# Key maxima as an activation bias, query maxima crossed by DMA, queries rounded by a reduction: an attention and feed-forward kernel on one core

## The chip, the cores and the metric

The kernel runs on one core of one Trainium2 chip. The metric is the device time of the whole program in microseconds, as the median of several runs. A profiled execution, recorded by the hardware, gives the start and the length of every instruction on the five engines: TensorE (PE, with its weight loads shown as PEld), VectorE (DVE), ScalarE (ACT), GpSimd (POOL) and SyncE (SP), which here only issues transfers.

## The reference

Attention with a feature map in place of the softmax, followed by two dense layers:

```python
def phi(x):                                   # x: [8, 8, 576, 64], w_phi: [64, 128]
    proj = np.einsum('bhsd,df->bhsf', x, w_phi)
    proj = proj - np.max(np.abs(proj), axis=-1, keepdims=True)
    return np.concatenate([np.exp(proj), np.exp(-proj)], axis=-1)
q_p, k_p = phi(q), phi(k)
kv = np.einsum('bhsf,bhsd->bhfd', k_p, v)
z = np.sum(k_p, axis=2)
num = np.einsum('bhsf,bhfd->bhsd', q_p, kv)
den = np.einsum('bhsf,bhf->bhs', q_p, z)[..., None] + 1e-06
x = (num / den)   # heads side by side: [4608, 512]
h = x @ w_in      # [512, 2048]
out = np.maximum(0.01 * h, h) @ w_out         # [2048, 512]
```

All in float32. For every token (key or query) the largest absolute value over its 128 projected features is subtracted before the exponentials. The second half takes the exponential of the negated difference, that is of maximum minus projection.

## The kernel before

The work of attention is cut into 32 pairs: a pair is two heads of one batch, and four pairs make a batch of 576 tokens. Pairs 0 to 3 have a route of their own (`first_k_phase`, `first_q_phase`). Pairs 4 to 31 go through `k_phase(i)` and `q_phase(i)`, generators that yield between their steps. `attention()` interleaves the key phase of pair i with the query phase of pair i - 1, step by step.

Precise matrix products are made of rounded ones: a float32 value is split into a rounded high part and the rest (`kph` and `kpl` from `ek`, `qh` and `ql` from `eq`, `gh` and `gl` from `g`), and each product is three matmuls. Before pair 8 (`nat` in the code, `NK` and `NN` being 8) the phases use float32 matmuls and no split.

The key phase goes over the tokens in three groups `g` (two chunks of 128 tokens, two more, and one of 64). Tokens lie on the partitions, features along the free axis, so a token's maximum `m4` is a VectorE reduction (L252), one column for each chunk and head. The subtraction of the maximum is `ksub` (through the helper at L72, on VectorE, VectorE and POOL in turn, as `ENG` says), two exponentials follow for each chunk on ScalarE (L262 and L263, `ek`), then the split and the matmuls into `kvp` (L224). At the end `kvh` and `kvl` are written for the query phase. `kvh` has one buffer, so this waits until the query phase before has read it.

The query phase has features on the partitions after its matmuls (L337, L338). A VectorE transpose of 32x32 blocks (L339) turns the features of each group of 32 partitions along the free axis (`tq`), and a reduction (L341) gives, for each of four partition groups, the maximum over its own 32 features: `m`, of 128 partitions by 2 heads by 18 blocks of tokens. The maximum of a token is that over the four groups, so `m` has to cross partitions: six small VectorE operations (L343 to L348) fold the upper half on the lower, then the second quarter on the first, and copy the result back to all four. Then come, for each head, the subtraction (L354), the transpose back (L356), the exponentials (L361, L362), the split into `qh` (a cast, in the helper at L69) and `ql`, the matmuls with `kvh` and `kvl` (L376 to L381), and the copies of numerator and denominator (L383, L384). A last part transposes the denominators, takes reciprocals and multiplies into `ring` (L387 to L390 and L72). `tq`, `m`, `ms`, `mb` and `rc` have one buffer each, so two query phases hardly overlap.

`ring` holds two batches of attention's output. The feed-forward layers take blocks of 256 tokens from it, 18 in all: `split(i)` makes `xh` and `xl`, `layer1` (L562 to L565) the 16 groups of 128 hidden features, each followed by an activation and a split (`g`, `gh`, `gl`), and `layer2` (L582 to L584) adds them up in `acc`, from where the result is copied and stored (L590). A block needs whole batches: block 4 the pairs up to 11, block 6 those up to 15. The weights are loaded and split between the first stage and about 210 us (`load_weights`, L169).

The order of instructions on each engine is fixed when the program is built. A planner runs through the work with priorities and its own estimate of each instruction's time; attention (`PA`) comes ahead of the weights (`PW`), and these ahead of the feed-forward layers (0). On the chip every engine, and SP's queue of transfers, then works through its list in that order, and each instruction waits for what it needs.

Of the kernel before, what the change touches and what calls it, by code (L numbers as in the profile page):

```python
# [9 lines left out]
F32 = mybir.dt.float32  # L10
# [3 lines left out]
AF = mybir.ActivationFunctionType  # L14
ALU = mybir.AluOpType
AX = mybir.AxisListType

P = 128
B, H, S, D = 8, 8, 576, 64
NP = H // 2  # L20
F = 128
# [23 lines left out]
def attention_moe_kernel(ctx: ExitStack, tc: tile.TileContext, q, k, v, vt, w_phi, w_in, w_out, out):  # L45
    nc = tc.nc
# [7 lines left out]
    def st(shape, dt, tag):  # L54
        return sp.tile(shape, dt, tag=tag, name=tag, bufs=BUFS.get(tag, 1))
# [8 lines left out]
    def copy_(key, o, i):  # L64
        e = pick(key) or "a"
        if e == "a":
            nc.scalar.copy(o, i)  # L67
        else:
            (nc.vector if e == "v" else nc.gpsimd).tensor_copy(o, i)  # L69

    def tt_(key, o, a, b, op):
        (nc.vector if pick(key) == "v" else nc.gpsimd).tensor_tensor(o, a, b, op=op)  # L72
# [132 lines left out]
    def k_phase(i):  # L205
        nat = i < NK
        rk, rv = kraw.pop(i)
        if not nat:
            ks = st([P, 2, S], F32R, "ks")
            for j in range(2):  # L210
                o, n = slice(64 * j, 64 * j + 64), slice(64 - 64 * j, 128 - 64 * j)
                copy_("kh", ks[o, j], rk[o])
                nc.vector.tensor_tensor(ks[n, j], rk[o], ks[o, j].bitcast(F32), op=ALU.subtract)  # L213
            vh, vl = values()
            copy_("vh", vh[:, :, 0:64], rv[:, :, 0:64])
            for r, c in ((slice(0, P), slice(0, 8)), (slice(64, P), slice(8, 10))):
                tt_("vl", vl[r, c], rv[r, c, 0:64], vh[r, c, 0:64].bitcast(F32), ALU.subtract)
        if i + 1 < B * NP:
            load_k(i + 1)
        yield  # L220
        kvp = pt("c")

        def kv_mm(j, lt, rt, first=False, last=False):
            nc.tensor.matmul(kvp[0 : lt.shape[1], 256 * j : 256 * j + 256], lhsT=lt, rhs=rt,  # L224
                             start=first and j == 0, stop=last, skip_group_check=True)

        for g in range(3):
            w = 2 if g < 2 else 1
            r = slice(0, P) if g < 2 else slice(64, P)
            n = P if g < 2 else 64  # L230
            m4 = st([P, 4], F32, "m4")
            pmk = st([P, 4, F], F32, "pmk")
            if nat:
                pk = pt("a")
                for s in range(w):
                    t0 = (2 * g + s) * P if g < 2 else S - P
                    proj(pk, s, rk[:, t0 : t0 + P])
                pkv = pk[r, 0 : 256 * w].rearrange("p (a f) -> p a f", f=F)
            else:
                for s in range(w):  # L240
                    t0 = (2 * g + s) * P if g < 2 else S - P
                    pk = pt("a")
                    for j in range(2):
                        nc.tensor.matmul(pk[:, 256 * j : 256 * j + 256], lhsT=ks[:, j, t0 : t0 + P],
                                         rhs=wq.rearrange("p a f -> p (a f)"), start=True, stop=True)
                    pk = pk[r].rearrange("p (j x f) -> p j x f", j=2, x=2)
                    x = pmk[r, 2 * s : 2 * s + 2]
                    copy_("pk", x, pk[:, :, 1])
                    nc.vector.tensor_tensor(x, pk[:, :, 0], x, op=ALU.add)
                    yield  # L250
                pkv = pmk[r, 0 : 2 * w]
            nc.vector.tensor_reduce(m4[r, 0 : 2 * w], pkv, axis=AX.X, op=ALU.max, apply_absolute_value=True)  # L252
            mb = m4[r, 0 : 2 * w].unsqueeze(2).broadcast_to([n, 2 * w, F])
            if nat:
                nc.vector.tensor_tensor(pmk[r, 0 : 2 * w], pkv, mb, op=ALU.subtract)
            else:
                tt_("ksub", pkv, pkv, mb, ALU.subtract)
            yield
            for s in range(w):
                c = 2 * g + s  # L260
                ek = st([P, 2, 256], F32, ("ek", "kph", "kpl")[c % 3] if nat else "ek")
                nc.scalar.activation(ek[r, :, 0:F], pmk[r, 2 * s : 2 * s + 2], AF.Exp)  # L262
                nc.scalar.activation(ek[r, :, F:256], pmk[r, 2 * s : 2 * s + 2], AF.Exp, scale=-1.0)  # L263
                if nat:
                    for j in range(2):
                        kv_mm(j, rv[r, 4 * j + c if c < 4 else 8 + j], ek[r, j], first=c == 0, last=c == 4)
                    yield
                    continue
                if c < 4:
                    kph = st([P, 2, 256], F32R, "kph")  # L270
                    kpl = st([P, 2, 256], F32R, "kpl")
                    copy_("kph", kph, ek)
                    tt_("kpl", kpl, ek, kph.bitcast(F32), ALU.subtract)
                    for j in range(2):
                        kv_mm(j, vh[:, 4 * j + c], kph[:, j], first=c == 0)
                        kv_mm(j, vl[:, 4 * j + c], kph[:, j])
                    for j in range(2):
                        kv_mm(j, vh[:, 4 * j + c], kpl[:, j])
                else:
                    kst = st([P, 2, 256], F32R, "kph")  # L280
                    copy_("kst", kst[r], ek[r])
                    nc.vector.tensor_tensor(kst[0:64], ek[r], kst[r].bitcast(F32), op=ALU.subtract)
                    for j in range(2):
                        kv_mm(j, vl[:, 8 + j], kst[:, j])
                        kv_mm(j, vh[:, 8 + j], kst[:, j], last=True)
                yield
        kvs = st([P, 2, 256], F32, "ek").rearrange("p a (b f) -> p a b f", b=2)[0:66]
        copy_("kvs", kvs, kvp[0:66].rearrange("p (a b f) -> p a b f", a=2, b=2))
        yield
        kvt = pt("c")  # L290
        kvtv = kvt[:, 0:264].rearrange("p (a b f) -> p a b f", a=2, b=2)
        for j in range(2):
            for t in range(2):
                nc.tensor.transpose(kvtv[:, j, t], kvs[:, j, t], ident[0:66, 0:66])
        if i < NN:
            kvh = st([P, 2, 2, P], F32, "kvh")
            nc.scalar.copy(kvh[:, :, :, 0:64], kvtv[:, :, :, 0:64])
            nc.scalar.copy(kvh[:, :, :, 64:P], kvtv[:, :, :, 64:65].broadcast_to([P, 2, 2, 64]))
            kvs_of[i] = kvh, None
        else:  # L300
            kvh = st([P, 2, 2, P], F32R, "kvh")
            kvl = st([P, 2, 2, P], F32R, "kvl")
            zb = kvtv[:, :, :, 64:65].broadcast_to([P, 2, 2, 64])
            copy_("kvh", kvh[:, :, :, 0:64], kvtv[:, :, :, 0:64])
            copy_("kvh", kvh[:, :, :, 64:P], zb)
            nc.vector.tensor_tensor(kvl[:, :, :, 0:64], kvtv[:, :, :, 0:64], kvh[:, :, :, 0:64].bitcast(F32), op=ALU.subtract)
            nc.vector.tensor_tensor(kvl[:, :, :, 64:P], zb, kvh[:, :, :, 64:P].bitcast(F32), op=ALU.subtract)
            kvs_of[i] = kvh, kvl
        yield
# [4 lines left out]
    def q_phase(i):  # L314
        b, hp = divmod(i, NP)
        nat = i < NN
# [12 lines left out]
        for j in range(2):  # L329
# [9 lines left out]
                nc.vector.transpose(tq[:, j, u], pq)  # L339
                yield  # L340
            nc.vector.tensor_reduce(m[:, j], blocks(tq[:, j]), axis=AX.X, op=ALU.max, apply_absolute_value=True)  # L341
        ms = st([64, 2, 18], F32, "ms")
        nc.vector.tensor_copy(ms, m[64:128])  # L343
        nc.vector.tensor_tensor(m[0:64], m[0:64], ms, op=ALU.max)
        nc.vector.tensor_copy(ms[0:32], m[32:64])
        nc.vector.tensor_tensor(m[0:32], m[0:32], ms[0:32], op=ALU.max)
        nc.vector.tensor_copy(m[32:64], m[0:32])
        nc.vector.tensor_copy(m[64:128], m[0:64])  # L348
        yield
        kvh, kvl = kvs_of[i]  # L350
        dn = tq[:, 0]
        for j in range(2):
# [6 lines left out]
            for u in range(2):  # L359
                eq = st([P, 2, U], F32, "eq")  # L360
                nc.scalar.activation(eq[:, 0], mb[:, u], AF.Exp)  # L361
                nc.scalar.activation(eq[:, 1], mb[:, u], AF.Exp, scale=-1.0)  # L362
                if nat:
                    es.append((eq, None))
                else:
                    qh = st([P, 2, U], F32R, "qh")
                    ql = st([P, 2, U], F32R, "ql")
                    copy_("qh", qh, eq)
                    tt_("ql", ql, eq, qh.bitcast(F32), ALU.subtract)
                    es.append((qh, ql))  # L370
                yield
# [307 lines left out]
```

## Time and profile before

| | us |
|---|---|
| Median of 3 runs | 1229.77 (1229.44 to 1230.68) |
| Profiled execution, its time | 1229.39 |
| its span, first to last instruction | 1227.6 |
| TensorE matmuls busy | 1179.4 (96%) |
| VectorE busy | 839.9 (68%) |
| ScalarE busy | 795.7 (65%) |
| POOL busy | 665.8 (54%) |
| TensorE clock granted, mean | 0.995 |

Busy times count an engine's instructions without its waits. Matmuls overlap one another, so 96% is not the share of the peak. Rows of groups read: line, engine, operation, output and inputs by the program's names, shapes, count, then busy us and mean ns, then the idle time before them and what ended it. Rows of a single line give shortest, median and longest in ns and the first and last start in us. L69 and L72 are helpers, so those rows are told apart by their tiles. SPq rows are issues of transfers by SP's queue.

### The profile page before, as it was taken

To read this page: it belongs to the slowest core of one execution; us is meant where nothing else is said; L and a number is where in the kernel's file an instruction comes from. 1 tells how busy PE (TensorE), PEld (TensorE's weight loads), DVE (VectorE), ACT (ScalarE), POOL (GpSimd) and SP (SyncE) were. 2 spreads that over 40 slices of the span, in tenths; PEclk is the share of its full clock that TensorE was granted. 3 is DMA by queue.
4 is the path that set the end of the run, shared out by engine and by line. 5 is a ranking of instruction groups with operands and counts; after the bars stand their busy time and mean duration, and the time that the engine had idled before them with its cause. 6 is when DMAs were issued, how large, how long until landed. Compare 5 with 4: busy or idle time off the path is not lost. (4 is left out here: it accounts for less than half of the span.)

```text
span 1227.6 us, 21133 instructions
## 1 busy us (share of the span) xinstructions
PE 1179.4 (96%) x7496; PEld 1033.1 (84%) x7496; DVE 839.9 (68%) x1359; ACT 795.7 (65%) x2027; POOL 665.8 (54%) x705
## 2 busy tenths in 40 slices
PE   8889999899998999999999999999999999999998
PEld 5577778788886889899898998889988889998997
DVE  6969995687887788888788888825888887200000
ACT  5977775776675676777777776745776766433232
POOL 0131222567665576768668785645677866433232
PEclk9999999999999999999999999999999999999999
DMA  7525231211111101111111111110111100000000
GB/s 211 147 75 174 82 105 30 75 30 32 38 31 48 31 28 41 30 40 32 48 32 48 24 47 30 42 28 29 30 49 31 35 14 1 19 18 1 18 18 18
DMA packets 62777, 57.00 MB, mean 46 GB/s; under 512 B 45136, under 2 KB 46288, under 8 KB 62672
## 3 DMA queue, kind: packets, MB, share of 16 engines
q1 hardware_dynamic: 62672, 55.65, 16.1%
q8 instruction: 59, 0.97, 0.3%
q14 instruction: 46, 0.38, 0.1%
HBM read 46.20 MB, written 9.44 MB: 45 GB/s over the span
## 5 line engine op out<-in xcount | busy, mean ns | idle before, releaser
L72 POOL TENSOR_TENSOR gl<-g,gh 128x256 fp32r<-128x256 f32 x288 | 242.0, 843 | 300.1 <-ACT gh L67 232.3
L562 PE MATMUL h<-xh,w0h 128*128 128x256 f32 x1088 | 278.4, 284 | 4.0 <-ACT xh L67 1.7
L563 PE MATMUL h<-xh,w0l 128*128 128x256 f32 x1088 | 276.3, 282 | 0.0
L562 PEld LDWEIGHTS h<-xh,w0h 128*128 128x128 f32 x1088 | 205.6, 189 | 16.1 <-ACT xh L67 2.3
L582 PE MATMUL acc<-w1h,gh 128*128 128x512 f32 x544 | 216.3, 398 | 2.2 <-DVE o L69 1.5
L583 PE MATMUL acc<-w1l,gh 128*128 128x512 f32 x544 | 214.8, 395 | 0.0
L563 PEld LDWEIGHTS h<-xh,w0l 128*128 128x128 f32 x1088 | 205.6, 189 | 8.6
L584 PE MATMUL acc<-w1h,gl 128*128 128x512 f32 x544 | 205.4, 396 | 1.2 <-POOL gl L72 1.2
L569 ACT ACTIVATE g<-h 128x256 f32<-128x256 f32 x288 | 109.1, 382 | 135.0 <-PE h L565 90.1
L72 POOL TENSOR_TENSOR ql<-eq,qh 128x576 fp32r<-128x576 f32 x96 | 154.8, 1618 | 65.9 <-DVE qh L69 57.4
L565 PE MATMUL h<-xl,w0h 128*128 128x256 f32 x1088 | 189.0, 283 | 0.3 <-POOL xl L72 0.2
L67 ACT CAST gh<-g 128x256 fp32r<-128x256 f32 x288 | 114.9, 403 | 66.2 <-PE acc L583 64.2
L565 PEld LDWEIGHTS h<-xl,w0h 128*128 128x128 f32 x1088 | 155.3, 190 | 2.4 <-POOL xl L72 1.9
L72 POOL TENSOR_TENSOR kpl<-ek,kph 128x512 fp32r<-128x512 f32 x72 | 102.2, 1420 | 38.2 <-ACT kph L67 17.2
L69 DVE CAST qh<-eq 128x576 fp32r<-128x576 f32 x96 | 97.2, 1016 | 36.0 <-ACT eq L362 22.7
L584 PEld LDWEIGHTS acc<-w1h,gl 128*128 128x128 f32 x544 | 100.1, 188 | 19.6 <-POOL gl L72 2.2
L582 PEld LDWEIGHTS acc<-w1h,gh 128*128 128x128 f32 x544 | 102.5, 188 | 16.2 <-DVE o L69 2.5
L583 PEld LDWEIGHTS acc<-w1l,gh 128*128 128x128 f32 x544 | 102.5, 188 | 11.5
L361 ACT ACTIVATE eq<-mb 128x288 f32<-128x288 f32 x112 | 49.2, 439 | 77.3 <-DVE mb L356 73.8
L69 DVE COPY o<-acc 128x512 f32<-128x512 f32 x16 | 10.7, 672 | 124.0 <-DMA out_dram<-o 124.0
L262 ACT ACTIVATE ek<-pmk 128x256 f32<-128x256 f32 (+1 forms) x128 | 53.4, 417 | 61.5 <-DVE pmk L72 19.6
L224 PE MATMUL c<-kph,vhl 128*66 128x256 f32 (+1 forms) x480 | 77.9, 284 | 6.1 <-ACT kph L67 3.3
(205 smaller groups left out, 2444.6 us busy)
## 6 DMA issues: line engine op xcount, KB each, us to landing
out_dram<-o SPq DMA_DIRECT2D x35, 256.0 KB, 2.0
rq<-in_q_dram SPq DMA_DIRECT2D x28, 288.0 KB, 2.9
rk<-in_k_dram SPq DMA_DIRECT2D x27, 288.0 KB, 2.8
rv<-in_v_dram SPq DMA_DIRECT2D x29, 256.0 KB, 3.5
ring<-in_w_in_dram SPq DMA_DIRECT2D x9, 512.0 KB, 3.9
f<-in_w_out_dram SPq DMA_DIRECT2D x7, 512.0 KB, 3.6
f<-in_w_in_dram SPq DMA_DIRECT2D x7, 512.0 KB, 3.7
ring<-in_w_out_dram SPq DMA_DIRECT2D x5, 512.0 KB, 3.6
```

Source lines behind the costliest of these rows:

```text
L67: nc.scalar.copy(o, i)
L69: (nc.vector if e == "v" else nc.gpsimd).tensor_copy(o, i)
L72: (nc.vector if pick(key) == "v" else nc.gpsimd).tensor_tensor(o, a, b, op=op)
L224: nc.tensor.matmul(kvp[0 : lt.shape[1], 256 * j : 256 * j + 256], lhsT=lt, rhs=rt, start=first and j == 0, stop=last, skip_group_check=True)
L262: nc.scalar.activation(ek[r, :, 0:F], pmk[r, 2 * s : 2 * s + 2], AF.Exp)
L562: nc.tensor.matmul(ph, lhsT=weight(0, "h", ft)[:, d * P : d * P + P], rhs=xh[d], start=d == 0, stop=False)
L563: nc.tensor.matmul(ph, lhsT=weight(0, "l", ft)[:, d * P : d * P + P], rhs=xh[d], start=False, stop=False)
L565: nc.tensor.matmul(ph, lhsT=weight(0, "h", ft)[:, d * P : d * P + P], rhs=xl[d], start=False, stop=d == NP - 1)
L569: nc.scalar.activation(g, ph, AF.Prelu, alpha=0.01)
L582: nc.tensor.matmul(a, lhsT=gh[:, ts], rhs=weight(1, "h", ft), start=ft == 0, stop=False)
L583: nc.tensor.matmul(a, lhsT=gh[:, ts], rhs=weight(1, "l", ft), start=False, stop=False)
L584: nc.tensor.matmul(a, lhsT=gl[:, ts], rhs=weight(1, "h", ft), start=False, stop=ft == NFT - 1)
```

## The change

In the key phase, from pair 8 on, the subtraction goes away. VectorE negates the maxima (`m4n`), and the exponentials take maximum or negated maximum as a bias per token, which needs an activation for each head: four of 128 elements for each chunk in place of two of 256. In the query phase of all pairs from 4 on, the four partition groups' maxima are brought side by side on 32 partitions by four transfers on SP's queue, reduced by one VectorE instruction, and sent to all four groups by four more transfers; `ms`, `mm` and `mx` have one buffer each, and there is one more yield. From pair 8 on the rounding of `eq` to `qh` is a VectorE maximum over an axis of one element instead of a cast.

```diff
@@ k_phase
             mb = m4[r, 0 : 2 * w].unsqueeze(2).broadcast_to([n, 2 * w, F])
+            if not nat:
+                m4n = st([P, 4], F32, "m4n")
+                nc.vector.tensor_scalar(m4n[r, 0 : 2 * w], m4[r, 0 : 2 * w], -1.0, None, op0=ALU.mult)
             if nat:
                 nc.vector.tensor_tensor(pmk[r, 0 : 2 * w], pkv, mb, op=ALU.subtract)
-            else:
-                tt_("ksub", pkv, pkv, mb, ALU.subtract)
             yield
             for s in range(w):
...
-                nc.scalar.activation(ek[r, :, 0:F], pmk[r, 2 * s : 2 * s + 2], AF.Exp)
-                nc.scalar.activation(ek[r, :, F:256], pmk[r, 2 * s : 2 * s + 2], AF.Exp, scale=-1.0)
+                if nat:
+                    nc.scalar.activation(ek[r, :, 0:F], pmk[r, 2 * s : 2 * s + 2], AF.Exp)
+                    nc.scalar.activation(ek[r, :, F:256], pmk[r, 2 * s : 2 * s + 2], AF.Exp, scale=-1.0)
+                else:
+                    for j in range(2):
+                        h = 2 * s + j
+                        nc.scalar.activation(ek[r, j, 0:F], pmk[r, h], AF.Exp, bias=m4n[r, h : h + 1])
+                        nc.scalar.activation(ek[r, j, F:256], pmk[r, h], AF.Exp, scale=-1.0, bias=m4[r, h : h + 1])
@@ q_phase
-        ms = st([64, 2, 18], F32, "ms")
-        nc.vector.tensor_copy(ms, m[64:128])
-        nc.vector.tensor_tensor(m[0:64], m[0:64], ms, op=ALU.max)
-        nc.vector.tensor_copy(ms[0:32], m[32:64])
-        nc.vector.tensor_tensor(m[0:32], m[0:32], ms[0:32], op=ALU.max)
-        nc.vector.tensor_copy(m[32:64], m[0:32])
-        nc.vector.tensor_copy(m[64:128], m[0:64])
+        ms = st([32, 4, 2, 18], F32, "ms")
+        for a in range(4):
+            nc.sync.dma_start(ms[:, a], m[32 * a : 32 * a + 32])
+        yield
+        mm = st([32, 2, 18], F32, "mm")
+        nc.vector.tensor_reduce(mm, ms.rearrange("p a j c -> p j c a"), axis=AX.X, op=ALU.max)
+        mx = st([P, 2, 18], F32, "mx")
+        for a in range(4):
+            nc.sync.dma_start(mx[32 * a : 32 * a + 32], mm)
+        m = mx
         yield
...
-                    copy_("qh", qh, eq)
+                    nc.vector.tensor_reduce(qh, eq.unsqueeze(3), axis=AX.X, op=ALU.max)
                     tt_("ql", ql, eq, qh.bitcast(F32), ALU.subtract)
```

## The prediction

> **What bounds the kernel now.** I read the page's busy shares first, then stages cut out of the trace, then what each engine waited for, then single stretches of the timeline.
>
> ```profile
> span 1227.6 us, 21133 instructions
> PE 1179.4 (96%) x7496; PEld 1033.1 (84%) x7496; DVE 839.9 (68%) x1359; ACT 795.7 (65%) x2027; POOL 665.8 (54%) x705
> ...
> 92.10:122.80 30.70, 30.70 (x173) 23.73 (x172) 28.40 (x56) 24.44 (x55) 5.82 (x9) 1.00 0.60 174
> 368.40:399.10 30.70, 25.40 (x145) 20.66 (x145) 22.59 (x37) 16.20 (x42) 17.27 (x20) 0.94 0.17 48
> 399.10:798.20 399.10, 388.40 (x2602) 350.02 (x2600) 338.31 (x515) 288.69 (x748) 282.27 (x270) 1.00 0.14 36
> 798.20:828.90 30.70, 29.85 (x203) 27.10 (x202) 8.27 (x12) 14.74 (x37) 15.12 (x17) 1.00 0.09 24
> ```
>
> The window rows give length, then PE, PEld, DVE, ACT, POOL busy (and counts), granted clock, DMA share, GB/s. TensorE is busy nearly throughout and its work is not touched, so by the shares alone the change could win at most the stalls. Two rows say more. From 798 to 829 VectorE falls to 8.27 of 30.70 us while PE goes on: attention has run ahead and waits for room in the ring. From 368 to 399 it is the other way: PE gets through 145 matmuls where the long stage after it has 2602 in 399.1 us, 200 in the same time, and its clock is granted at 0.94. There PE is short of tokens:
>
> ```profile
> 235.28 1.42 POOL L72 TENSOR_TENSOR ring<-ring,mb 128x576 f32<-128x576 f32 x1 [2.17 <-ACT o L67]
> 236.84 0.35 ACT L67 CAST xh<-ring 128x192 fp32r<-128x192 f32 x1
> 380.07 1.41 POOL L72 TENSOR_TENSOR ring<-ring,mb 128x576 f32<-128x576 f32 x1 [0.20 <-DVE mb L390]
> 381.51 0.30 ACT L67 CAST xh<-ring 128x128 fp32r<-128x128 f32 x1 [0.22 <-POOL ring L72]
> 381.87 0.39 PE L562 MATMUL h<-xh,w0h 128*128 128x256 f32 x1 [1.02 <-ACT xh L67]
> 515.00 1.43 POOL L72 TENSOR_TENSOR ring<-ring,mb 128x576 f32<-128x576 f32 x1
> 516.46 0.24 ACT L67 CAST xh<-ring 128x64 fp32r<-128x64 f32 x1 [0.80 <-POOL ring L72]
> ```
>
> The last product of pair 7, of pair 11 and of pair 15 is split for the feed-forward layers the moment it is there (236.84, 381.51, 516.46), and at 381.87 PE waited for that split. So up to pair 15 the end of each batch of attention paces PE; later PE paces attention, with the 30 us pause at 798 as slack.
>
> Attention's own pace is that of the query phase. It has one `tq`, so a pair starts when the one before is done:
>
> ```profile
> 1035.33 0.48 DVE L339 STREAM_TRANSPOSE tq<-a 128x288 f32<-128x288 f32 x1
> 1057.49 0.78 DVE L390 STREAM_TRANSPOSE mb<-rc 128x576 f32<-128x576 f32 x1
> L390 DVE STREAM_TRANSPOSE mb<-rc x28: 728/778/779, 133.7 to 1057.5; 128x576 f32<-128x576 f32 x28
> ```
>
> The last transposes (L390) of 28 query phases lie 27 steps apart from 133.7 to 1057.5 us: 34.2 us a pair, about 33.1 without the pause. Pair 31, the only one with no key phase beside it, takes 1035.3 to 1058.3, 23 us. So some 10 us a pair are lost to sharing engines with the next pair's keys.
>
> **The change, part by part.** The rows are those of 245 to 1045 us (pairs 8 to 31, nearly).
>
> ```profile
> L72 DVE TENSOR_TENSOR pmk<-pmk,m 128x512 f32<-128x512 f32 x46 | 41.9, 910 | 0.7
> L72 POOL TENSOR_TENSOR pmk<-pmk,m 64x256 f32<-64x256 f32 x23 | 16.1, 699 | 24.7 <-DVE m L252 18.6 <-PE a L244 2.4 <-ACT tq L384 2.4
> L262 ACT ACTIVATE ek<-pmk 128x256 f32<-128x256 f32 x92 | 38.5, 418 | 38.9 <-DVE pmk L72 19.6 <-POOL kpl L72 18.6
> L67 ACT CAST xh<-ring 128x128 fp32r<-128x128 f32 x16 | 3.7, 296 | 0.2 <-POOL ring L72 0.2
> L345 DVE COPY ms<-m x28: 170/172/1200, 109.1 to 1039.6; 32x36 f32<-32x36 f32 x28
> L343 DVE COPY ms<-m 64x36 f32<-64x36 f32 x24 | 9.0, 373 | 0.4
> L345 DVE COPY ms<-m 32x36 f32<-32x36 f32 x24 | 11.3, 470 | 0.8
> L348 DVE COPY m<-m 64x36 f32<-64x36 f32 x24 | 8.9, 370 | 0.8
> L69 DVE CAST qh<-eq 128x576 fp32r<-128x576 f32 x96 | 97.2, 1016 | 36.0 <-ACT eq L362 22.7
> L69 DVE CAST qh<-eq x96: 434/907/1702, 257.1 to 1049.5; 128x576 fp32r<-128x576 f32 x96
> L341 DVE TENSOR_REDUCE m<-tq x56: 702/749/756, 96.8 to 1038.4; 128x18 f32<-128x576 f32 x56
> ```
>
> *Keys.* Per pair the subtraction goes: 2 of 0.91 us on VectorE and one of 0.70 us on POOL. In its place come 3 negations `m4n` of 2 or 4 columns. The nearest row is the small copy L345: 0.17 us at best and in the middle, 0.47 on average over the stage, up to 1.2 when something holds it up. I take 0.4, so VectorE gains 1.8 - 1.2 = 0.6 us a pair (bounds 0.4 and 1.3). ScalarE goes from 2 instructions a chunk of 256 elements (0.418 each) to 4 of 128 (0.296 for a 128-element cast): 1.18 for 0.84, +0.35 a chunk, +1.7 us a pair of 5 chunks. ScalarE has 288.69 of 399.1 us busy, 24 us a pair, so it can carry that; it lies in the key phase, which waits for the query phase at `kvh`. Price 0 on the path. The Trainium skill ("ScalarE: Activation LUTs", section "What ACT_TABLE_LOAD costs") adds about 93 ns for a bias read per partition; no row here has one. By it the surcharge would be about 3.6 us a pair, an estimate from that page, and ScalarE still not full.
>
> *Rounding of the queries.* 4 casts a pair, 0.43 to 1.70 us, median 0.91, mean 1.02, become reductions. A reduction over the same 576 elements costs 0.75 us and hardly varies. -0.27 us each, -1.1 a pair on the query path from pair 8 on; an undisturbed cast (0.43) loses 0.3 each, so the bounds are -1.1 and +1.2.
>
> *The crossing.* Out go the six small operations L343 to L348, 0.37 to 0.47 us each on average (first, dearest and last are shown), together 2.46 us of VectorE a pair, in all 28 pairs. In come 4 DMAs, a reduction of 144 elements on 32 partitions (between the 0.17 us of a small copy and the 0.75 of 576 elements; I take 0.3), 4 DMAs. Both hops lie on the query path: `m` to `ms` to `mm` to `mx` to L354. All eight go through SP's queue; behind them stand the loads of the next pair and the stores of the output.
>
> ```profile
> rv<-in_vt_dram SPq DMA_DIRECT2D x58, 32.0 KB, 2.9
> out_dram<-o SPq DMA_DIRECT2D x35, 256.0 KB, 2.0
> L191 SPq DMA_DIRECT2D rk<-in_k_dram x26: 327/334/436, 12.9 to 964.8; - x26
> L193 SPq DMA_DIRECT2D rv<-in_vt_dram x28: 658/662/1505, 23.5 to 977.6; - x28
> 388.62 0.34 SPq L200 DMA_DIRECT2D rq<-in_q_dram  x1
> 391.02 0.56 SPq L192 DMA_DIRECT2D rv<-in_v_dram  x1
> 391.63 0.67 SPq L193 DMA_DIRECT2D rv<-in_vt_dram  x1
> 388.52 0.71 DVE L343 COPY ms<-m 64x36 f32<-64x36 f32 x1
> 391.49 0.18 DVE L348 COPY m<-m 64x36 f32<-64x36 f32 x1
> ```
>
> SP spends 0.33 to 0.66 us on an issue, and a transfer lands 2.0 (the stores) to 2.9 us (the smallest loads) after its issue starts. The last of four issues starts 3 x 0.33 = 1.0 to 3 x 0.66 = 2.0 us after the first, so a hop is 3.0 to 4.9 us; I take 4.0, the middle. Crossing: 2 x 4.0 + 0.3 = 8.3, bounds 6.3 and 10.1. Pair 12's crossing (388.52 to 391.67) falls together with the loads for the next pair on SP (388.62 to 392): a load waiting for its buffer holds the small DMAs behind it, and they hold the loads. I add 1 us: 9.3 in place of 2.5 of work, +6.8 on the path.
>
> While the hop runs, VectorE is free for the key phase. That gives back part of the 10 us of sharing. I take 3.5, half of the 6.8 us hole: VectorE is busy for 28 us a pair (338.31 of 399.1 us, 33.1 a pair), but the hole can only take key work that is ready in it. So from pair 8: +6.8 - 1.1 - 3.5 - 0.6 = +1.6 us a pair (bounds -2 and +6).
>
> Pairs 4 to 7 have no rounding gain, VectorE stays full there (28.40 of 30.70 at 92 us), and SP's queue also feeds the weights, whose loads wait for staging room:
>
> ```profile
> SPq L169 <- DVE ql L177: 66.7, 22, 5.8
> PE a L376 <- DVE qh L69: 4.3, 8, 0.9
> PE a L337 <- DVE tq L339: 3.1, 4, 1.3
> PE c L224 <- POOL kpl L72: 2.4, 6, 0.8
> ```
>
> That is 3 us for each of 22 loads (66.7 in total). The hole there is filled with weight work, which PE needs too. I take +3.5 us a pair, half of the 6.8 (bounds 0 and +10, with a 3 us load ahead of each hop).
>
> **The sum.** Up to pair 15 this reaches PE: 4 x 3.5 + 8 x 1.6 = 27 us. From there 16 x 1.6 = 26 us fits into the 30 us pause. What comes back: PE stalls on VectorE and POOL (4.3 + 3.1 + 2.4 us in the last rows and smaller ones), and slowed chains once PE itself runs short; I take -8. Span 1227.6 + 27 - 8 = 1246.6. The profiled execution took 1229.39, 1.8 over its span and 0.4 under the median of 1229.77: 1248.4, on the median's scale 1248.8. I say 1248.
>
> **The rivals.** *The hop is short and VectorE's relief decides (faster).* VectorE loses 2.46 - 0.3 + 1.1 + 0.6 = 3.9 us of its 28 a pair. If the crossing takes 6.3 us, the lower bound, and the key work fills the hole, the path loses 3.8 - 1.1 - 3.5 - 0.6 = -1.4 us a pair. The first 12 pairs can give at most what PE lost waiting for tokens: between 368 and 399 some 55 matmuls of 0.15 us, 8.4 us, and less at pairs 7 and 15. With the 8 of stalls that is 1230 - 17 = 1213; about half of it, 1221, is likelier. For it: the six small operations cost 2.46 us where six undisturbed ones (0.17) would cost 1.0, so much of VectorE's time is waiting that goes with them. It decides once the crossing is below some 7.7 us, where the +1.6 above is used up. The Trainium skill ("SBUF — State Buffer", section "Who interferes with whom") has a copy, a cast and a two-input operation fight POOL for a shared port, and a reduction never; the trace agrees (casts 0.43 to 1.70, reductions 0.70 to 0.76), and by that rule alone the change should win. By the same page the negations can still be held up. Chance 0.29.
>
> *It all hides (same).* The key work fills the hole exactly and PE, 96% busy, sees nothing: within 2.5 us, 0.2%, about what a measurement of this kernel can tell from no change. Against it: pairs 7, 11 and 15. Chance 0.08.
>
> *VectorE's order does not leave the room (much slower).* Engines run in a fixed order. If the reduction on `ms`, and L354 on `mx`, stand in VectorE's order 2 us too early each, everything behind them waits: the key phase's L249, the transposes L339, then PE. +4 us a pair over my +1.6: 5.6 x 12 = 67 in the first half plus the part of 90 in the second that the pause of 30 does not take, partly repaid as PE's shortage frees ScalarE and POOL: some 1265 to 1320, by how much of it is repaid. Nothing here shows how the order reckons with a small DMA. Chance 0.18.
>
> **How the numbers follow.** Likeliest: the crossing lengthens attention moderately, 1233 to 1265, chance 0.45, at 1248 (the likeliest case's own range). Slower is 0.45 + 0.18 = 0.63, same 0.08, faster 0.29. For 8 in 10 I cut the lower part of the fast case (below 1214) and the upper part of the slow one (above 1290): 1214 to 1290.
>
> **What would show it.** Right: VectorE's total near 840 - 28 x 2.2 - 96 x 0.27 - 14 = 738 us; the `qh` reductions at 0.75 us; ScalarE up by 40 to 90 us; from the end of the second L341 to L354 8 to 11 us; 35 to 36 us a pair; PE's clock dipping near pairs 7, 11 and 15 for longer than now. Wrong: a crossing under 7 us, or pairs that follow each other in 32 us, would make it faster; `mm` waiting on SP behind loads for 5 us and more, or VectorE idle at `mm` and L354 with key work behind it, much slower.

## The result and the profile after

The changed kernel takes 1221.51 us (median of 5 runs), the kernel before 1230.68 in the same series: a ratio of 0.9926, 95% interval 0.9913 to 0.9939. I had forecast 1248, slower. The profiled execution has a span of 1217.5 us, 10.1 less than before.

The page of the changed kernel, and below it the stages (length, then PE, PEld, DVE, ACT, POOL busy with counts, granted clock, DMA share, GB/s), first of the kernel before, then of the changed one:

```profile
span 1217.5 us, 21546 instructions
PE 1171.4 (96%) x7496; PEld 1038.5 (85%) x7496; DVE 741.7 (61%) x1243; ACT 865.7 (71%) x2267; POOL 625.2 (51%) x681
```

```profile
214.90:245.60 30.70, 27.49 (x165) 23.22 (x164) 21.28 (x37) 21.96 (x59) 15.62 (x23) 0.94 0.25 75
245.60:552.60 307.00, 294.18 (x1937) 262.83 (x1936) 251.32 (x382) 214.89 (x558) 204.66 (x203) 0.99 0.13 35
552.60:798.20 245.60, 238.57 (x1606) 214.66 (x1604) 210.23 (x323) 176.98 (x458) 176.61 (x166) 1.00 0.14 38
...
828.90:1043.80 214.90, 209.97 (x1415) 190.74 (x1415) 169.60 (x270) 148.15 (x392) 147.23 (x147) 1.00 0.10 27
```

```profile
214.90:245.60 30.70, 22.04 (x101) 15.95 (x99) 15.40 (x29) 21.38 (x57) 10.20 (x17) 0.83 0.26 76
245.60:552.60 307.00, 290.13 (x1907) 262.60 (x1908) 205.84 (x344) 238.06 (x640) 189.73 (x193) 0.97 0.13 35
552.60:798.20 245.60, 245.34 (x1683) 226.64 (x1683) 173.45 (x275) 196.06 (x529) 159.95 (x158) 1.00 0.14 38
798.20:828.90 30.70, 30.70 (x215) 28.47 (x214) 22.30 (x38) 24.45 (x66) 20.31 (x19) 1.00 0.13 32
828.90:1043.80 214.90, 214.40 (x1469) 198.18 (x1468) 149.04 (x242) 170.12 (x464) 140.30 (x146) 1.00 0.12 32
```

In the changed kernel's rows later lines have moved: its L572 is the L562 of before, its L348 the L341, its L364 the L354.

The counts of matmuls say where the time went, since both kernels run the same 7496. (They are of several sizes; weighed by size, as an estimate from the trace, the two sums below come to 11 and 22 us.) Up to 552.6 us the changed kernel is behind: 101 + 1907 for 165 + 1937, 94 fewer. After that it is ahead: 1683 + 215 + 1469 for 1606 + 203 + 1415, 143 more. In a full slice PE does 215 in 30.70 us, 0.143 us each. So some 13 us were lost up to about pair 15 and some 20 were won after it; the remaining 3 lie before 215 us and in the tail. The slice from 798 to 829, where attention had paused before, is an ordinary one now (VectorE 22.30 us for 8.27).

The loss is where the prediction looked for it. The last product of pairs 7, 11 and 15 and the split and matmul that wait for it, in the changed kernel's timeline:

```profile
250.31 1.42 POOL L72 TENSOR_TENSOR ring<-ring,mb 128x576 f32<-128x576 f32 x1
...
252.16 0.39 PE L572 MATMUL h<-xh,w0h 128*128 128x256 f32 x1 [0.81 <-ACT xh L67]
...
389.30 1.40 POOL L72 TENSOR_TENSOR ring<-ring,mb 128x576 f32<-128x576 f32 x1
...
391.08 0.39 PE L572 MATMUL h<-xh,w0h 128*128 128x256 f32 x1 [0.74 <-ACT xh L67]
...
528.00 1.41 POOL L72 TENSOR_TENSOR ring<-ring,mb 128x576 f32<-128x576 f32 x1
530.12 0.23 ACT L67 CAST xh<-ring 128x64 fp32r<-128x64 f32 x1
530.40 0.58 PE L572 MATMUL h<-xh,w0h 128*128 128x256 f32 x1 [1.84 <-ACT xh L67]
```

These products came at 235.28, 380.07 and 515.00 before: 15, 9 and 13 us later now, and PE waits for the split at all three. Its granted clock in the slice from 215 to 246 is 0.83, where it was 0.94.

The crossing of pair 13 in VectorE's timeline, before and after:

```profile
422.77 0.75 DVE L341 TENSOR_REDUCE m<-tq 128x18 f32<-128x576 f32 x1
423.56 0.18 DVE L343 COPY ms<-m 64x36 f32<-64x36 f32 x1
...
425.56 0.65 DVE L345 COPY ms<-m 32x36 f32<-32x36 f32 x1
426.25 1.23 DVE L346 TENSOR_TENSOR m<-m,ms 32x36 f32<-32x36 f32 x1
...
428.60 0.75 DVE L354 TENSOR_TENSOR tq<-tq,m 128x576 f32<-128x576 f32 x1
```

```profile
428.67 0.75 DVE L348 TENSOR_REDUCE m<-tq 128x18 f32<-128x576 f32 x1
...
433.15 0.41 DVE L354 TENSOR_REDUCE mm<-ms 32x36 f32<-32x144 f32 x1 [2.16 <-DMA ms<-m]
...
437.18 1.02 DVE L364 TENSOR_TENSOR tq<-tq,mx 128x576 f32<-128x576 f32 x1 [0.62 <-DMA mx<-mm]
```

From the end of the second reduction to the subtraction it was 5.1 us and is 7.8. Over pairs 16 to 23 the means are 4.8 and 8.4 us. Before, the small operations were done in fits: two of them took 0.65 and 1.23 us in this pair for work that takes 0.17 undisturbed. What POOL did at that time, in the kernel before:

```profile
425.44 0.73 POOL L72 TENSOR_TENSOR gl<-g,gh 128x256 fp32r<-128x256 f32 x1 [1.77 <-ACT gh L67]
426.14 1.29 POOL L72 TENSOR_TENSOR kpl<-ek,kph 128x512 fp32r<-128x512 f32 x1
```

The first of the two slow ones ends at 426.21 us, POOL's `gl` at 426.17; the second at 427.48, POOL's `kpl` at 427.43. It is so throughout the trace. Of the 112 small copies of the crossing 73 start while no POOL instruction runs, and take 0.17 to 0.18 us. Of the 39 others 37 take longer, up to 1.34 us, and 36 of these end within 0.1 us of the POOL instruction that was running. In the changed kernel VectorE stands idle for the transfers instead (2.16 and 0.62 us).

The groups of the new instructions in the changed kernel (busy us, mean ns of one, then the idle time before them and its releasers):

```profile
L269 ACT ACTIVATE ek<-pmk,m4n 128x128 f32<-128x128 f32 x192 | 72.0, 394 | 37.3 <-POOL kpl L72 23.1 <-DVE m4n L256 13.8
L378 DVE TENSOR_REDUCE qh<-eq 128x576 fp32r<-128x576 f32 x96 | 70.0, 750 | 42.6 <-ACT eq L372 23.3 <-PE a L388 10.7 <-ACT g L579 3.6
L256 DVE TENSOR_SCALAR m4n<-m 128x4 f32<-128x4 f32 x48 | 19.2, 400 | 0.8
```

The transfers of the crossing's first hop, as SP issues them (ns: shortest, median, longest), and then in the view of the DMA issues, which ends with the median us from issue to landing:

```profile
L351 SPq DMA_DIRECT2D ms<-m x112: 507/588/1565, 105.2 to 1046.4; - x112
```

```profile
ms<-m SPq DMA_DIRECT2D x112, 4.5 KB, 1.7
```

### The profile page after: what moved, and what is told of

Read it like the earlier page. It is cut to its first block, busy times and chain, and to the rows that moved or that the text cites. A ratio compares the mean times of both kernels' runs of the same rounds, so it can differ in the third digit from the quotient of the medians.

```text
span 1217.5 us, 21546 instructions
## 1 busy us (share of the span) xinstructions
PE 1171.4 (96%) x7496; PEld 1038.5 (85%) x7496; DVE 741.7 (61%) x1243; ACT 865.7 (71%) x2267; POOL 625.2 (51%) x681
## 4 chain that ended last, share of the span: by engine, by line
PE 72%; ACT 8%; DVE 6%; issue 4%; DMA 3%; POOL 3%; SPq 2%; DVEq 0%; POOLq 0%; ACTq 0%
PE h L572 9%; PE h L575 9%; PE h L573 9%; PE acc L592 8%; PE acc L593 8%; PE acc L594 8%; PE c L224 6%; PE a L386 2%; PE a L244 2%; PE a L391 2%; PE a L388 2%; DMA ring<-in_w_in_dram 1%; DMA ms<-m 1%; PE a L344 1%; PE a L345 1%
## 5 line engine op out<-in xcount | busy, mean ns | idle before, releaser
L72 POOL TENSOR_TENSOR gl<-g,gh 128x256 fp32r<-128x256 f32 x288 | 233.7, 816 | 314.7 <-ACT gh L67 251.9
L572 PE MATMUL h<-xh,w0h 128*128 128x256 f32 x1088 | 281.3, 286 | 7.4 <-ACT xh L67 4.1
L573 PE MATMUL h<-xh,w0l 128*128 128x256 f32 x1088 | 278.2, 283 | 0.0
L572 PEld LDWEIGHTS h<-xh,w0h 128*128 128x128 f32 x1088 | 206.9, 190 | 20.4 <-ACT xh L67 5.1
L575 PE MATMUL h<-xl,w0h 128*128 128x256 f32 x1088 | 192.2, 283 | 0.0
L72 POOL TENSOR_TENSOR ql<-eq,qh 128x576 fp32r<-128x576 f32 x96 | 146.7, 1537 | 51.6 <-DVE qh L378 39.3
L72 POOL TENSOR_TENSOR kpl<-ek,kph 128x512 fp32r<-128x512 f32 x72 | 97.2, 1350 | 80.2 <-ACT kph L67 46.5
L269 ACT ACTIVATE ek<-pmk,m4n 128x128 f32<-128x128 f32 (+1 forms) x240 | 88.4, 393 | 44.4 <-POOL kpl L72 23.1
L270 ACT ACTIVATE ek<-pmk,m 128x128 f32<-128x128 f32 (+1 forms) x240 | 88.0, 391 | 25.3 <-DVE m L252 20.8
L378 DVE TENSOR_REDUCE qh<-eq 128x576 fp32r<-128x576 f32 x96 | 70.0, 750 | 42.6 <-ACT eq L372 23.3
L249 DVE TENSOR_TENSOR pmk<-a,pmk 128x256 f32<-128x256 f32 (+1 forms) x120 | 48.3, 417 | 50.5 <-ACT pmk L67 47.9
```

The costliest lines, as they stand in the source:

```text
L269: nc.scalar.activation(ek[r, j, 0:F], pmk[r, h], AF.Exp, bias=m4n[r, h : h + 1])
L270: nc.scalar.activation(ek[r, j, F:256], pmk[r, h], AF.Exp, scale=-1.0, bias=m4[r, h : h + 1])
L572: nc.tensor.matmul(ph, lhsT=weight(0, "h", ft)[:, d * P : d * P + P], rhs=xh[d], start=d == 0, stop=False)
L573: nc.tensor.matmul(ph, lhsT=weight(0, "l", ft)[:, d * P : d * P + P], rhs=xh[d], start=False, stop=False)
L575: nc.tensor.matmul(ph, lhsT=weight(0, "h", ft)[:, d * P : d * P + P], rhs=xl[d], start=False, stop=d == NP - 1)
```

## The experiments

Three theories stood at the start. Theory 1: PE's stalls go because VectorE and POOL no longer hold each other up. Theory 2: the slower crossing itself helps, since attention no longer runs ahead and its work is spread evenly. Theory 3: the planner's order is a matter of luck, and any edit moves it. All ratios are to the kernel before, with their 95% intervals.

**The parts alone, and an edit that changes only the order.**

`e1_keys`: the hunks of the change in the key phase alone.

> Only the key part of the change: from pair 8 on no subtraction, the maximum as a bias. Theory 1 (PE's stalls go because VectorE no longer holds up POOL and is held up by it): the 42 us of VectorE and 16 us of POOL subtractions go, the negations cost some 29 us (0.40 us each in the changed kernel), so a gain of 3 to 6 us. Theory 2 (the slower crossing evens out attention's pace, so that PE is never short of filler after pair 15): no part but the crossing can win; within 2.5 us, with the pause of attention near 800 us still there. Theory 3 (any edit gives the planner another order, and orders differ by about 10 us): anything, with no relation to the other parts.

Measured: 1237.92 us, 1.0053 (1.0041 to 1.0065), slower. The part that takes the most work from VectorE and POOL in the key phase loses when alone. VectorE falls to 805.8 us busy and ScalarE rises to 858.5. That is against theory 1, which had a gain of 3 to 6 us. The query phase from L354 to the first transpose of its last part (L387) takes 21.0 us in pairs 16 to 23, where it took 19.0.

`e2_cross`: the hunk of the crossing alone.

> Only the crossing by eight small DMAs, in all pairs from 4 on. Theory 1: the longer crossing (8.4 us for 5.0 in the changed kernel) costs some 10 us up to pair 15 and 2.5 us of VectorE a pair comes back as fewer stalls, so about 0 to +8 us. Theory 2: most of the 9 us gain of the whole change, 3 to 9 us faster, and the pause near 800 us gone. Theory 3: anything.

Measured: 1236.34, 1.0048 (1.0036 to 1.0060). Against theory 2, which had a gain of 3 to 9 us; the time lies in theory 1's range.

`e3_round`: the rounding alone.

```diff
-                    copy_("qh", qh, eq)
+                    nc.vector.tensor_reduce(qh, eq.unsqueeze(3), axis=AX.X, op=ALU.max)
```

> Only the rounding of the queries by a reduction, from pair 8 on. Theory 1: casts of 0.43 to 1.70 us become reductions of 0.75 us; PE's waits for qh (4.3 us) and part of those for ql (1.6 us) go and the query phase is 1 us a pair shorter, so a gain of 3 to 8 us. Theory 2: within 2.5 us. Theory 3: anything.

Measured: 1230.43, 0.9996 (0.9986 to 1.0007). Nothing in the total, though pair 15 ends at 505.6 us, 9 us earlier than before.

`e4_yield`: order alone.

```diff
         nc.vector.tensor_copy(m[64:128], m[0:64])
         yield
+        yield
```

> The kernel before with one more yield after the crossing and nothing else: the same instructions, possibly in another order. It measures what a new order alone is worth. Theories 1 and 2: within 3 us of before. Theory 3: 5 to 12 us away from before, on either side.

Measured: 1229.38, 0.9989 (0.9981 to 0.9998), though the order did change on every engine. No part alone wins, two lose half a per cent, and yet together they win 0.74%.

**Two parts at a time.** `e5_keys_round`, `e6_cross_round` and `e7_keys_cross` are the change without its crossing, keys and rounding hunks.

> The whole change without the crossing: keys and rounding. Alone the keys cost +6 us, the rounding nothing, the crossing +6. If the gain of 9 us comes from VectorE and POOL alone (theory 1), this is faster than the whole change, 1210 to 1220, as it is spared the longer crossing in the pairs up to 15. If the crossing is what makes the others pay (theory 2), about the sum of the two alone, 1234 to 1240.

> The whole change without the keys: crossing and rounding. Theory 1: 1230 to 1238, as VectorE still has the subtractions. Theory 2 (attention's pace decides, the keys only load ScalarE): 1216 to 1230. If effects simply add up: 1236.

> The whole change without the rounding: keys and crossing. If effects add up, 1243. If the keys' relief of VectorE is what fills the holes of the crossing (the two together pay, the rounding does nothing, as it does alone), 1219 to 1226. If the order is chance (theory 3), anywhere from 1215 to 1245.

| rounding | neither | keys | crossing by DMA | keys and crossing |
|---|---|---|---|---|
| without | 1 | 1.0053 | 1.0048 | 1.0019 (1.0011 to 1.0028) |
| with | 0.9996 | 0.9957 (0.9945 to 0.9969) | 0.9946 (0.9933 to 0.9958) | 0.9926 |

Of these three kernels `e5_keys_round` lies between the ranges of theories 1 and 2, `e6_cross_round` in theory 2's, and `e7_keys_cross` outside what the first two forecasts for it said.

The rounding is worth 0.9 to 1.0% beside either of the others and nothing without them. In the keys kernel it brings pair 31's end from 1080.9 to 1061.8 us, in the crossing kernel from 1089.0 to 1078.2. I read this so: where attention is late, a shorter query path counts; in the kernel before, where attention even pauses, it does not. No run isolates it, and the granted clock may be another part of it. In the median it is 0.995 before, 0.988 with the keys alone, 0.986 with the crossing or the rounding alone, 0.984 with the whole change. In the eleven runs of `e3_round` it goes from 0.990 (1227.18 us) to 0.981 (1233.63 us), some 0.7 us for each 0.001. By that estimate 5 to 6 us of each of the three kernels with one part go with the clock: most of what keys and crossing lose alone, and a gain that the rounding alone may have made and lost again. In the traces the clock falls in slices where PE runs short of matmuls (0.78 from 368 to 399 us in `e3_round`, 0.83 from 215 to 246 in the changed kernel), so it may be a result of the late tokens and no cause of its own; no run separates the two.

**The early pairs.** `e8_late8`: the whole change, but pairs 4 to 7 keep the six small operations.

```diff
+        if i < 8:
+            ... the six operations of before, on a tile of their own
+        else:
+            ... the crossing by DMA
```

> The whole change, but pairs 4 to 7 keep the six small VectorE operations for the crossing; the DMAs begin at pair 8. In the changed kernel pair 7 ends 14 us later than before (249.4 for 235.1) and PE's clock falls to 0.83 in the slice from 215 to 246. If that is the longer crossing of pairs 4 to 7, pair 7 comes back to 235 to 240 and the kernel gains 8 to 14 us over the changed one: 1208 to 1214. If pairs 4 to 7 are held by the weights, no change: 1219 to 1224.

Measured: 1225.88, 0.9960 (0.9948 to 0.9972): 0.3% slower than the whole change and outside both ranges, though pair 7 did come back, to 240.9 us for 249.4. The first two stages of this kernel:

```profile
214.90:245.60 30.70, 25.22 (x138) 20.63 (x137) 17.07 (x31) 22.93 (x64) 13.82 (x21) 0.90 0.26 75
245.60:552.60 307.00, 288.27 (x1890) 261.28 (x1890) 211.42 (x338) 235.09 (x633) 187.71 (x191) 0.96 0.13 35
```

PE does 138 matmuls for 101 in the first of them, and 1890 for 1907 in the second. Pair 11 ended at 388.6 against 388.4. The 8.5 us were gone four pairs later. I suppose that a late attention meets a PE with little else to do, and is quicker for it; no run tests that.

**Delay without relief, relief without delay.** `e9_delay` keeps the six operations and adds one hop of four transfers.

```diff
         nc.vector.tensor_copy(m[64:128], m[0:64])
+        mx = st([P, 2, 18], F32, "mx")
+        for a in range(4):
+            nc.sync.dma_start(mx[32 * a : 32 * a + 32], m[32 * a : 32 * a + 32])
+        m = mx
```

> The kernel before with a longer crossing and no relief: after the six small VectorE operations, m goes through four more DMAs into mx, some 3.5 us a pair (a hop of the changed kernel), while VectorE's work stays at 840 us. Theory 2 (a slower attention alone lets PE run full after pair 15): PE at 30.7 of 30.7 us in most slices from 552 on, the pause near 800 us gone, 1226 to 1236 in all. Theory 1 (the relief of VectorE does it): the slices after 552 stay as ragged as before, and the loss up to pair 15 comes on top: 1238 to 1250.

`e10_reduce` replaces the six operations by nine reductions, and has no transfer.

```diff
+        ms = st([32, 4, 2, 18], F32, "ms")
+        for a in range(4):
+            nc.vector.tensor_reduce(ms[:, a], m[32 * a : 32 * a + 32].unsqueeze(3), axis=AX.X, op=ALU.max)
+        mm = st([32, 2, 18], F32, "mm")
+        nc.vector.tensor_reduce(mm, ms.rearrange("p a j c -> p j c a"), axis=AX.X, op=ALU.max)
+        mx = st([P, 2, 18], F32, "mx")
+        for a in range(4):
+            nc.vector.tensor_reduce(mx[32 * a : 32 * a + 32], mm.unsqueeze(3), axis=AX.X, op=ALU.max)
+        m = mx
```

> The kernel before with the crossing made of VectorE reductions alone, none of which POOL holds up: four reductions over one element bring the groups side by side on 32 partitions, one takes the maximum, four bring it back, nine of 0.17 to 0.4 us, about 2 us in a row without a transfer. Theory 1: VectorE busy 815 to 830 us, pairs as quick as before or quicker, 3 to 8 us faster than before. Theory 2: no gain, within 3 us, as the pause of attention near 800 us stays.

Measured: the delay 1240.48, 1.0081 (1.0064 to 1.0098); the reductions 1210.31, 0.9830 (0.9817 to 0.9844). The stages after 552 us, first with the delay, then with the reductions:

```profile
552.60:798.20 245.60, 238.14 (x1600) 215.21 (x1598) 190.84 (x293) 167.12 (x434) 164.46 (x160) 1.00 0.13 35
798.20:828.90 30.70, 28.66 (x195) 25.88 (x194) 24.63 (x41) 19.18 (x51) 16.68 (x17) 1.00 0.12 32
828.90:1043.80 214.90, 208.77 (x1400) 189.22 (x1400) 163.95 (x254) 147.87 (x391) 144.73 (x149) 1.00 0.11 30
```

```profile
552.60:798.20 245.60, 242.92 (x1671) 225.15 (x1670) 209.33 (x330) 179.39 (x461) 177.31 (x169) 1.00 0.14 38
798.20:828.90 30.70, 30.70 (x203) 28.05 (x203) 10.67 (x26) 15.31 (x43) 13.92 (x21) 1.00 0.06 20
```

With the delay the pause is gone (VectorE 24.63 us in the slice at 798), just as in the changed kernel, and PE is no fuller than before: 1600 matmuls for 1606. Theory 2 falls. With the reductions the pause is there (10.67) and PE does 1671. The matmuls from 552.6 to 1043.8 us, in one count for each kernel:

| kernel | matmuls | against before |
|---|---|---|
| before | 3219 | |
| `e4_yield`, order alone | 3180 | -39 |
| `e9_delay` | 3191 | -28 |
| `e1_keys` | 3214 | -5 |
| `e2_cross` | 3280 | +61 |
| `e10_reduce` | 3286 | +67 |
| `e6_cross_round` | 3331 | +112 |
| the change | 3362 | +143 |

`e2_cross` and `e10_reduce` both have no copy and no maximum of two inputs in the crossing, and fill PE by about the same, whether the maxima travel by DMA or not. Up to 552 us `e2_cross` does 112 fewer than before. An order alone moves the count by 39, so the smaller steps say little, and 61 and 67 stand not far above it. The amount of VectorE's work does not decide, since the reductions leave it where it was:

```profile
PE 1164.3 (97%) x7496; PEld 1032.1 (86%) x7496; DVE 843.4 (70%) x1443; ACT 796.4 (66%) x2027; POOL 672.7 (56%) x705
```

The first reductions of the crossing in that kernel (ns: shortest, median, longest):

```profile
L344 DVE TENSOR_REDUCE ms<-m x112: 170/178/184, 107.4 to 1017.9; 32x36 f32<-32x36 f32 x112
```

Theory 1 as I had put it, by the amount, falls with that; it had 3 to 8 us for this run, and the gain is 21. Left of it is that the crossing is not held up: 0.170 to 0.184 us for each of these pieces, where the copies took 0.17 to 1.34.

**The whole change with the crossing by reductions, and order again.** `e11_keys_round_reduce` has e10's crossing with keys and rounding; `e12_after_yield` is the changed kernel with one more yield.

> The whole change with the crossing made of VectorE reductions instead of DMAs. Theory 1: it has nearly the relief of VectorE and POOL (VectorE 755 to 775 us busy) without the longer path, so pair 7 ends near 238 us, pair 31 by 1060, and the kernel comes to 1205 to 1216, faster than the changed one. Theory 2: attention runs ahead again, the pause comes back, 1219 to 1228.

> The changed kernel with one more yield after the crossing: the same instructions in another order, to see what a new order is worth there. Theories 1 and 2: within 3 us of the changed kernel, 1218 to 1225. Theory 3 (the gain is a lucky order): 1226 or more.

Measured: 1209.56, 0.9822 (0.9809 to 0.9834), better than the change by 1.0%. The extra yield: 1217.14, 0.9885 (0.9871 to 0.9899), 0.4% off the change with the same instructions. So order alone has moved these kernels by up to 0.4%, and nothing smaller is read as an effect of a part; the 0.3% of `e8_late8` is not one.

**Hold-ups alone.** `e13_six` changes only the kind of four instructions in the program's text.

```diff
-        nc.vector.tensor_copy(ms, m[64:128])
+        nc.vector.tensor_reduce(ms, m[64:128].unsqueeze(3), axis=AX.X, op=ALU.max)
         nc.vector.tensor_tensor(m[0:64], m[0:64], ms, op=ALU.max)
... (the other three copies likewise)
```

> The kernel before with its six small operations, of which the four copies are made as reductions over one element; the two maxima of two inputs stay. Same count, same order of steps, same transfers. If hold-ups by POOL in the crossing are what costs (a copy takes 0.17 to 1.3 us, a reduction of this size 0.17 to 0.18), about half of the 21 us of the crossing by reductions: 1216 to 1224. If the hold-up only moves to the next operation with two inputs or a copy, or if the amount of VectorE work counts: 1227 to 1233.

Measured: 1216.55, 0.9883 (0.9869 to 0.9897). In this kernel's trace the copies made as reductions, and one of the two maxima that stayed, read:

```profile
L343 DVE TENSOR_REDUCE ms<-m x56: 177/180/186, 106.8 to 1026.1; 64x36 f32<-64x36 f32 x28, 32x36 f32<-32x36 f32 x28
L347 DVE TENSOR_TENSOR m<-m,ms x28: 181/230/1173, 108.2 to 1025.9; 64x36 f32<-64x36 f32 x28
```

Same steps, same data, same transfers, and 1.2% less time. The reductions are even, also the 59 of 112 that start while a POOL instruction runs (0.177 to 0.186 us); the maximum of two inputs is still held up now and then. The four copies took 41.2 us of VectorE in all before and take 20.2 as reductions, and the kernel gains 15. This is the plainest evidence that the hold-ups in the crossing cost time. The granted clock is the same (0.995, and 0.994 before). One rival is left: the planner gave PE, VectorE, ScalarE and POOL another order here too. Against it stands that the edits of order alone moved a kernel by 0.4% at most.

**What the other parts are worth then.** `e14_round_reduce` is e10 with the rounding, `e15_keys_reduce` e10 with the keys, `e16_reduce_yield` e10 with one more yield.

> Crossing by reductions and rounding by reduction, keys as before. The rounding was worth 11 to 12 us beside the keys or the crossing by DMA, and nothing alone. If it pays where attention is not held up elsewhere: 1196 to 1204, the fastest so far. If it pays only where attention is late: 1207 to 1213 as without it.

> Crossing by reductions and the key part, rounding as before. Alone the key part cost 6 us, since the query phase from L354 on became 2 us a pair longer (21.0 for 19.0, with ScalarE 63 us fuller). If that holds here too: 1214 to 1220. If the keys only hurt because of the held-up crossing: 1205 to 1212.

> The crossing by reductions with one more yield: the same instructions in another order. If its 21 us are the mechanism's: 1206 to 1215. If they are a lucky order: 1216 or more.

Measured: 1204.89, 0.9786 (0.9772 to 0.9800), the fastest of all; 1223.59, 0.9948 (0.9934 to 0.9963); 1212.69, 0.9853 (0.9839 to 0.9867). The first lies just above the range forecast for a rounding that pays, the second above both of its ranges, the third in the range for the mechanism. The crossing's gain survives another order. The key part costs 1.2% on top of e10, more than it did alone; the rounding adds 0.4%, no more than an order may. The best version keeps the old keys.

## Why the prediction was wrong

Two terms of the sum failed, one by 12 us or more and one by 14. With either one alone put right the sum would still have said slower, 1234 or 1236; with both it says 1222.

**Right.** Attention up to pair 15 paces PE, and the last products of pairs 7, 11 and 15 came 15, 9 and 13 us later, with PE's clock down near them. The 30 us pause took up the delay after that. VectorE was to fall to 738 us and stands at 741.7, the `qh` reductions at 0.750, the negations at 0.40, ScalarE 70 us higher (40 to 90 forecast), the crossing at 8.4 us (8 to 11). The pace was not the one named: 34.8 us a pair from pair 7 to 15 in place of 35 to 36.

**One step that failed: "What comes back ... I take -8".** PE got back some 20 us after 552 (143 matmuls of 0.143 us). I had read that term off three rows of PE's waits (4.3 + 3.1 + 2.4) and some for the rest. All the listed waits of PE from 552.6 to 1043.8 us come to 11.7 us before and 0.6 in the changed kernel, about half of what came back. A row that I had quoted said more: PE did 200 matmuls in 30.7 us of the long stage. In the changed kernel, where it is busy for 245.34 of 245.60 us from 552 on, it does 1683, which is 210 in the same time. That is 5%, some 23 us over 552 to 1044 (an estimate), and the change got nearly all of it. So "later PE paces attention" held only in part. The runs show what stood behind it: in part the kind of the crossing's operations (`e13_six`, 1.2%; `e10_reduce`, 1.7%; 61 of the 143 matmuls with the crossing alone, `e2_cross`), not the pace of attention (`e9_delay`) and not VectorE's total. The other 82 matmuls came only with the rounding and the keys beside it, and why is open.

**The other, mis-sized: "from pair 8: ... +1.6 us a pair".** I set the new crossing against the 2.46 us in which VectorE was busy with the old one. On the path the old one took some 5 us, as other work stood between its pieces and POOL held some of them up, so from pair 8 on the crossing added 3.4 to 3.7 and not 6.8. From pair 7's end to pair 15's end the changed kernel took 278.2 us (249.4 to 527.6), the kernel before 279.6: -0.2 us a pair. The early loss was 13 us in place of 27. For pairs 4 to 7, +3.5 a pair was right (14.3 us in all). My bounds on a hop were wrong at one end: the small transfers land in 1.7 us, below the 2.0 of the nearest row.

**Wrong: keys at "price 0 on the path".** Alone they cost 0.53%, most of it by the clock's estimate above; on e10 they cost 1.2%, at the same clock (0.994 for both). I took 0.296 us for a 128-element activation, from a cast without a bias; with one it is 0.394. The sentence from the Trainium skill ("ScalarE: Activation LUTs", "What ACT_TABLE_LOAD costs": about 93 ns for a bias read per partition) was the better guide: it gave 3.6 us a pair, and 5 x (4 x 0.392 - 0.84) = 3.6 is what the rows show. That the dearer activations hold up the query phase's own is argued from its longer second part in `e1_keys`; no run isolates it.

**The rival that came true** was "VectorE's relief decides", with 1221 us. Its own condition, a crossing under 7.7 us, was not met (8.4), and its amount of relief is not the cause; that the time came within 1 us of its 1221 is luck. The rule named beside it was: by the Trainium skill ("SBUF — State Buffer", "Who interferes with whom") copies, casts and two-input operations can compete with POOL and reductions never do. The trace agrees, 0.170 to 0.184 us for reductions against 0.17 to 1.34 for copies. I had given the rival a chance of 0.29.

**Open.** How a hold-up of a microsecond on VectorE turns into lost PE time is argued only: each engine works through a fixed order made from estimates that, I suppose, know of no hold-up, so one late step makes several engines wait in turn. In e10 the hold-ups moved in part to other operations (the subtractions `kpl`, `qs` and `ks` on VectorE took 21 us more in all than before) and it won all the same, so where they fall seems to matter; which place costs what was not tried. Nor is it settled why keys and crossing, each a loss alone, are less of one together (1.0019).

## What to carry to other kernels

Where VectorE and POOL both work from SBUF, a copy or a cast on the critical chain can be written as a reduction over an axis of one element. Undisturbed it costs the same at 36 elements (0.18 us) and more at 576 (0.75 us for 0.43), and no run here shows it held up, where the copy went to 1.34 and the cast to 1.70 us. With the copies this paid (`e13_six`); with the cast it gained nothing alone (`e3_round`). Set a new path against the elapsed time of the old one in the timeline, not against the busy time of its instructions. And size PE's hidden loss by the count of matmuls in a stage against one where PE is full with the same mix, not by the list of waits alone. The mix counts: in `e10_reduce` PE is busy for all of the slice from 798 to 829 us, where attention pauses, and does 203 matmuls, not 215.

## What I had not expected of the hardware

Transfers of 4.5 KB between partitions land 1.7 us after their issue (1.6 to 4.0), but SP takes 0.51 to 1.57 us, median 0.59, to issue each, so four in a row cost about as much in issuing as in flight. And what attention gains early need not last: 8.5 us won by pair 7 in `e8_late8` were gone by pair 11.
